# Attention with a gated MLP behind it: the first batch's LayerNorm spread tile by tile over two slots, and weight splits and copies placed elsewhere

## The chip, the cores and the metric

The kernel runs on one core of one Trainium2 chip, as one program. The metric is device time in microseconds: the median of several executions. Beside it stands one execution taken with the hardware profiler, from which all rows below come. TensorE is called PE there, VectorE DVE, ScalarE ACT, GpSimd POOL and SyncE SP. All loads and stores of this kernel but one are issued by SP.

## The reference

Block-causal attention over 8 batches of 8 heads (sequence 576, head size 64), then a gated MLP on its output:

```
scores = q @ k.T / 8, masked by blocks of 64; attn = softmax(scores); x = attn @ v     # (8, 576, 512)
h = gelu_tanh(x @ w_in)                  # w_in 512 x 1024
u, v = h[..., :512], h[..., 512:]
v_n = (v - mean(v)) / sqrt(var(v) + 1e-6) * g_ln          # over the last axis
v_s = einsum('ts,bsd->btd', w_sg, v_n) + b_sg[None, :, None]   # w_sg 576 x 576
out = x + (u * v_s) @ w_out
```

`w_in` and `w_out` come in as 64-bit floats, everything else as 32-bit floats.

## The kernel before

**Arithmetic.** Products that need 32-bit accuracy are made of three matmuls: each operand is split into a high part (a copy rounded to the matmul's 32-bit format, `fp32r`) and a low part (the difference). So `x` has `xh` and `xl`, the weights have `wi_h` and `wi_l`, `wo_h` and `wo_l`, `ws_h` and `ws_l`. Weights of 64 bits are first turned into 32-bit ones by bit operations: for a pair of 128x256 blocks, two passes of ACT, then five of DVE, then two of POOL for the split. `load_weight` yields after each of these three parts; `weight_half` runs one part. The spatial weights (`ws`, five blocks) only need POOL's two passes; the last of the five also holds the bias row, with one pass of ACT and one of DVE.

**Slots.** A slot is one pair of heads of one batch; there are 32, four for a batch. In slot n, PE turns the probabilities of pair n (`turn`: tiles `pA`, `pB`, `pC`, copied to `ptA`, `ptB`, `ptC`; `turn_sums`: `pd`, `pe`, copied to `rb`), makes half of the scores of pair n+1 (`first`), the product with the values (`products`: `ob`), the other half of the scores (`second`), and in four holes between these the tiles of the feed-forward part (FF) of the batch before: `v_part` (five tiles `accv`), `u_part` (eight `accu`), `s_part` (eight `accs`) and `o_part` (eight `acco`). DVE takes the maxima of the scores (`negm`), ACT the exponents (`prob`), POOL splits q and k of pair n+2.

Slots 0 to 3 (`opening_slot`) have no FF. The first batch's FF lies in slots 4 to 7 (`middle_slot`): the v tiles in slot 4, u in slots 5 and 6, s in slot 7. What else runs there, and after which hole, is written out in `SCRIPT`: `script[0]`, `[1]` and `[2]` come after the first three holes, `[3]` and `[4]` around the split of q and k, `[5]` at the slot's end. `weigh(k)` runs k parts of the weights' work, `fetch(k)` issues the loads of the next k weight blocks, `run_side(k)` k steps of the LayerNorm, `run_gelu` a waiting Gelu.

**Order.** In the first eight slots every engine runs its instructions in the order in which the program writes them, so an instruction that waits holds all that is behind it on its engine. From slot 8 on only PE's order is fixed, and the framework's scheduler orders the others by its own estimate of times.

**Buffers.** All matmuls write to a pool of eight PSUM banks (`bank`); a new tile takes a bank whose last reader is done, or waits for one. One pass of the weights' conversion takes a bank too. `KINDS` gives the buffers in SBUF: the five v tiles and the high and low parts of the normalised ones share nine, the raw spatial blocks `xr` have two, `x` has two.

**LayerNorm.** For each of five row tiles: `moments` (DVE, two instructions), `centre` (DVE: subtract the mean, multiply by the gain); then `inverse_std` for all tiles at once (POOL, two instructions); then `scale` (ACT makes the high part, DVE the low one; for the tail tile three instructions of DVE, which also write `vone`). `vone` is an operand whose lower half is all ones, for the bias.

All instructions go through the small class `Engine`, so most rows of the profile have its line, L60; the tiles' names tell them apart.

Of the kernel before, what the change touches and what calls it, by code (L numbers as in the profile page):

```python
# [9 lines left out]
F32 = mybir.dt.float32  # L10
# [10 lines left out]
def kernel(  # L21
# [13 lines left out]
    B, H, D, S = qT.shape  # L35
# [41 lines left out]
    def page(dtype, n, name):  # L77
        tag, bufs = KINDS.get(name, KINDS["w"])
        return sp.tile([P, n], dtype, tag=tag, name=name, bufs=bufs)
# [106 lines left out]
    ws_l = cp.tile([P, NT, S], F32R, name="ws_l")  # L186
    g_bc = cp.tile([P, DH], F32, name="g_bc")
    vone = cp.tile([P, DH], F32R, name="vone")

    def split_weight(x, dh, dl):  # L190
        gpsimd.tensor_copy(dh, x)
        gpsimd.tensor_tensor(dl, x, dh.bitcast(F32), op=ALU.subtract)

    W = 256
    raws = deque()
    coming = deque()

    def fetch(k=1):
# [4 lines left out]
    def fetch_weight(src, c, fs, name):  # L203

        t = page(src.dtype, W, name)
        sync.dma_start(t, src[c * P : (c + 1) * P, fs])
        raws.append(t)

    def fetches(src, cols, name):
        for f in range(cols.start, cols.stop, W):  # L210
# [3 lines left out]
    def load_weight(src, off, cols, dh, dl, name, size):  # L214

        parts = [(c, f) for f in range(0, cols, W) for c in range(NC)]
        for k in range(0, len(parts), size):
            c, f = parts[k]
            f += off
            if size == 2:  # L220
                dst = [x[:, c : c + 2, f : f + W] for x in (dh, dl)]
            else:
                dst = [x[:, c, f : f + W] for x in (dh, dl)]
                if coming:
                    fetch()
            raw = [raws.popleft() for _ in range(size)]
            if src.dtype == F32:
                yield False
                yield False
                for j, x in enumerate(raw):  # L230
                    split_weight(x, dh[:, c + j, f : f + W], dl[:, c + j, f : f + W])
                yield True
                continue
            words = [x.bitcast(U32).rearrange("p (n t) -> p n t", t=2) for x in raw]
            if size == 2:
                m = page(U32, size * W, name)
            else:
                tm = sp.tile([P, 2 * W], U32, tag="pt", name="tm", bufs=5)
                t, m = tm[:, :W], tm[:, W:]
            for j, x in enumerate(words):  # L240
                scalar.activation(
                    m[:, j * W : (j + 1) * W].bitcast(F32),
                    x[:, :, 1].bitcast(F32),
                    AF.Abs,
                    scale=2.0**-112,
                )
            yield False
            if size == 2:
                t = page(U32, size * W, name)
                y = bank("w").bitcast(U32)  # L250
            else:
                y = t
            for j, x in enumerate(words):
                yj = y[:, j * W : (j + 1) * W]
                vector.tensor_scalar(yj, x[:, :, 0], 29, None, op0=ALU.logical_shift_right)
                vector.scalar_tensor_tensor(
                    yj, x[:, :, 1], 0x80000000, yj, op0=ALU.bitwise_and, op1=ALU.bitwise_or
                )
            vector.scalar_tensor_tensor(
                t, m, 3, y, op0=ALU.logical_shift_left, op1=ALU.bitwise_or  # L260
            )
            yield False
            t = t.bitcast(F32)
            if size == 2:
                t = t.rearrange("p (c n) -> p c n", c=size)
            split_weight(t, *dst)
            yield True

    def load_spatial():
        t = page(F32, S, "x")  # L270
        gpsimd.memset(t[BLK:, :DH], 1.0)
        vector.tensor_copy(vone[BLK:, :], t[BLK:, :DH])

        for j in range(NT - 1):
            split_weight(raws.popleft(), ws_h[:, j, :], ws_l[:, j, :])
            yield True

        j = NT - 1
        t, t2 = raws.popleft(), raws.popleft()
        gpsimd.tensor_copy(ws_h[:, j, :], t)  # L280
        gpsimd.tensor_tensor(
            ws_l[:BLK, j, :], t[:BLK, :], ws_h[:BLK, j, :].bitcast(F32), op=ALU.subtract
        )
        scalar.copy(ws_l[BLK:, j, :], t2[BLK:, :])
        vector.tensor_tensor(
            ws_l[96:97, j, :], t2[96:97, :], ws_l[96:97, j, :].bitcast(F32), op=ALU.subtract
        )
        yield True

    def fetch_spatial(j):  # L290
        t = page(F32, S, "xr")
        sync.dma_start(t, w_sgT[j * P : (j + 1) * P, :])
        raws.append(t)

    def fetch_ends():
        t = page(F32, S, "xr")
# [3 lines left out]
        gpsimd.memset(t2[BLK:, :], 0.0)  # L300
        sync.dma_start(t2[BLK : BLK + 1, :], b_sg.unsqueeze(0))
        sync.dma_start(t2[96:97, :], b_sg.unsqueeze(0))
        raws.extend((t, t2))

    def fetch_gain():
        sync.dma_start(g_bc, g_ln.unsqueeze(0).broadcast_to([P, DH]))
# [140 lines left out]
    class Values:  # L447
# [75 lines left out]
        def split(self):  # L523

            x = self.x
            hi, lo = page(F32R, S + TAIL, "xh"), page(F32R, S, "xl")
            vector.tensor_copy(hi[:, :S], x)
            gpsimd.tensor_tensor(
                hi[:, S:], x[:, S - TAIL :], hi[:, S - TAIL : S].bitcast(F32), op=ALU.subtract
            )  # L530
# [2 lines left out]


    side = deque()

    def run_side(k):

# [29 lines left out]
    def v_part(b, vv, vn, vn_t, u, g_s):  # L568
        need("v")
        x_s = xs[b]  # L570
        for st in range(NT):
# [15 lines left out]
            else:  # L587
                vt = sp.tile([P, DH], F32, tag="pt", name="vt", bufs=5)
                scalar.copy(vt[:TAIL, :], acc[BLK:, :])
                vector.tensor_tensor(x, acc[:TAIL, :], vt[:TAIL, :], op=ALU.add)  # L590
            yield "v"
        rs = sp.tile([P, NT], F32, tag="rs", name="rs", bufs=2)

        def moments(st):
# [33 lines left out]
                )  # L628

        side.append(("G", lambda: gelu(vv, last)))  # L630
        for st in range(NT):
            side.append(("V", lambda st=st: moments(st)))
        side.append(("V", inverse_std))
# [1 line left out]
            side.append(("V", lambda st=st: centre(st)))  # L635
        for st in (NT - 1, *range(NT - 1)):
            side.append(("V", lambda st=st: scale(st)))

    def u_part(b, vv, vn, vn_t, u, g_s):
        need("u")  # L640
# [111 lines left out]
    def opening_slot(n, va):  # L752
# [34 lines left out]
        if n == Q - 1:  # L787
            nv.inverse()
            split_qk(n + 2)
        return nx, nv  # L790

    def slot(n, va):
# [44 lines left out]
        return nx, nv  # L837

    def weigh(k=1):
        for _ in range(k):  # L840
            weight_half()

    SCRIPT = {
        4: (
            lambda: (fetch(2), weigh(1)),
            lambda: weigh(3),
            lambda: (fetch(2), weigh(3)),
            lambda: None,
            lambda: weigh(3),
            lambda: (fetch(3), weigh(2)),  # L850
        ),
        5: (
            lambda: (run_gelu(), weigh(1), fetch(1)),
            lambda: run_side(2),
            lambda: (run_side(3), weigh(1), fetch(1)),
            lambda: run_side(1),
            lambda: weigh(1),
            lambda: None,
        ),
        6: (  # L860
            lambda: (run_side(5), weigh(1), fetch(1)),
            lambda: (run_side(4), weigh(1)),
            lambda: run_side(1),
            lambda: None,
            lambda: fetch(1),
            split_pending,
# [11 lines left out]
    def middle_slot(n, va):  # L878
# [6 lines left out]
        va.turn("A1")  # L885
        if n != 2 * Q - 2:
            split_pending()
        hole(g[0])
        script[0]()
        va.turn("B0")  # L890
# [12 lines left out]
        if n % Q == Q - 1:  # L903
            va.split()
        else:
            pending.append(va.split)
        nv = Values(n + 1, nx)
        nv.inverse()
        script[3]()
        split_qk(n + 2)  # L910
        script[4]()
        hole(g[3])
# [6 lines left out]
    split_qk(0)  # L919
    load_qk(1)  # L920
    fetch(2)
    sc = Scores(0)
    sc.first()
    sc.second()
# [58 lines left out]
```

## Time and profile before

| | |
|---|---|
| median of 3 runs | 750.47 us (750.12 to 751.44) |
| the profiled execution | 748.33 us, of it a span of 746.5 us from first to last instruction |
| granted TensorE clock, mean | 0.995 |
| busy PE / DVE / ACT / POOL | 732.5 / 469.3 / 429.2 / 295.2 us |
| PE's longest waits | `ob` for ACT's `ptC` 3.1 us, `s` for DVE's `negm` 1.2, `s` for DVE's `ptB` 1.1, `accv` for POOL's `xl` 0.6 us |
| slots 4 to 7 | from about 52 to 140 us |

A row of the timeline has the start in us, the duration, engine, line, operation, tiles written and read, shape, a count where several were merged, and in brackets the idle time of the engine before it with what ended that. A row of the windows has, for each engine, its busy time and instructions in the stretch, then the granted clock, the DMA engines' mean busy share and GB/s.

### The profile page before, as it was taken

Reading aid. Unit: us, or ns where it says so; the run is one execution under the profiler, and the core shown is the slowest. Engines: PE = TensorE matmul, PEld = TensorE weight load, DVE = VectorE, ACT = ScalarE, POOL = GpSimd, SP = SyncE. Lnnn points to the kernel's source line nnn. Section 1 sums busy time; section 2 is a strip of 40 time slices with the busy share of each in tenths; the row PEclk is TensorE's granted clock in tenths of the full one; section 3 lists DMA queues with packets and bytes.
Section 4 is the critical chain, followed back from the end, with each engine's and each line's share of the span. In section 5 each row is a group of like instructions: output and inputs, shape, how many; then the busy total and the mean of one; then the engine's idle time right before and its main releaser. Section 6 shows DMA issues by size and latency. Waiting matters only on the chain.

```text
span 746.5 us, 18406 instructions
## 1 busy us (share of the span) xinstructions
PE 732.5 (98%) x6936; PEld 689.4 (92%) x6936; DVE 469.3 (63%) x1461; ACT 429.2 (57%) x1072; POOL 295.2 (40%) x360
## 2 busy tenths in 40 slices
PE   8999979999999999999999999999999999999998
PEld 6888879999998999989999899998999989998997
DVE  5997797778963487634866449554595446941732
ACT  6987768378632785437754487445873476722500
POOL 3866755645333343423435123452224432322121
PEclk9999989999999999999999999999999999999999
DMA  6566433334341223312252123521224221220032
GB/s 166 172 170 192 110 80 88 112 92 140 95 134 42 72 72 120 118 35 69 84 176 66 47 58 95 160 72 40 75 79 149 72 71 41 80 79 2 10 120 95
DMA packets 84299, 70.04 MB, mean 94 GB/s; under 512 B 59890, under 2 KB 59890, under 8 KB 84212
## 3 DMA queue, kind: packets, MB, share of 16 engines
q1 hardware_dynamic: 84068, 68.58, 31.6%
q8 instruction: 55, 0.90, 0.5%
q10 hardware_dynamic: 144, 0.29, 0.1%
q14 instruction: 32, 0.26, 0.1%
HBM read 49.98 MB, written 18.87 MB: 92 GB/s over the span
## 4 chain that ended last, share of the span: by engine, by line
PE 84%; DVE 7%; ACT 5%; issue 2%; DMA 1%; POOL 0%; ACTq 0%; DVEq 0%; POOLq 0%
PE accs L60 16%; PE acco L60 13%; PE accv L60 12%; PE accu L60 11%; PE s L60 10%; PE ob L60 10%; ACT prob L60 4%; PE pA L60 3%; PE pB L60 3%; PE pd L60 3%; PE pC L60 2%; DVE prob L60 2%; PE pe L60 1%; DVE vv L604 1%; DVE bs L598 1%
## 5 line engine op out<-in xcount | busy, mean ns | idle before, releaser
L60 ACT ACTIVATE prob<-prob,negm 128x576 f32<-128x576 f32 (+3 forms) x320 | 176.4, 553 | 60.1 <-DVE negm L60 58.8
L60 DVE CUSTOM_DVE_ANT_0 prob<-s,mask 128x256 f32<-128x256 f32 (+3 forms) x320 | 119.3, 417 | 44.0 <-PE s L60 41.4
L60 POOL TENSOR_TENSOR xh<-x,xh 128x64 fp32r<-128x64 f32 x32 | 10.5, 328 | 195.8 <-DVE xh L60 167.2
L60 POOL TENSOR_TENSOR gl<-u,gh 128x288 fp32r<-128x288 f32 x64 | 52.0, 816 | 90.2 <-DVE gh L60 73.9
L60 PE MATMUL accu<-xh,wi_h 128*128 128x288 f32 x256 | 78.3, 306 | 0.0
L60 PE MATMUL acco<-gh,wo_h 128*128 128x288 f32 x256 | 77.5, 303 | 0.4 <-DVE negm L60 0.2
L60 PE MATMUL accs<-ws_h,vh 128*128 128x288 f32 x256 | 77.9, 304 | 0.0
L60 PE MATMUL accs<-ws_h,vl 128*128 128x288 f32 x256 | 75.5, 295 | 0.0
L60 PE MATMUL accu<-xl,wi_h 128*128 128x288 f32 x256 | 75.5, 295 | 0.0
L60 PE MATMUL accs<-ws_l,vh 128*128 128x288 f32 x256 | 75.4, 295 | 0.0
L60 PE MATMUL acco<-gh,wo_l 128*128 128x288 f32 x256 | 75.4, 295 | 0.0
L60 PE MATMUL acco<-gl,wo_h 128*128 128x288 f32 x256 | 75.4, 295 | 0.0
L60 PE MATMUL accu<-xh,wi_l 128*128 128x288 f32 x256 | 75.4, 295 | 0.0
L60 PE MATMUL s<-kh,qh 64*128 64x320 f32 (+4 forms) x384 | 63.6, 321 | 3.4 <-ACT kh L60 1.2
L60 PE MATMUL accv<-wi_h,xh 128*128 128x512 f32 x160 | 65.3, 408 | 0.0
L60 DVE TENSOR_TENSOR u<-accs,u 128x288 f32<-128x288 f32 x64 | 29.2, 456 | 56.8 <-PE accs L60 55.1
L60 PE MATMUL accv<-wi_l,xh 128*128 128x512 f32 x160 | 62.8, 393 | 0.0
L60 ACT ACTIVATION_READ_ACCUMULATOR prob<-prob,negm 128x1 f32 x320 | 59.9, 187 | 0.0
L60 PE MATMUL s<-kh,ql 64*128 64x320 f32 (+4 forms) x384 | 59.1, 300 | 0.0
L60 PE MATMUL s<-kl,qh 64*128 64x320 f32 (+4 forms) x384 | 58.0, 299 | 0.3 <-DVE kl L60 0.3
L60 ACT COPY vv<-accv 128x512 f32<-128x512 f32 x32 | 18.6, 582 | 64.9 <-PE accv L60 64.9
L60 POOL CAST kh<-k_f 128x576 fp32r<-128x576 f32 x31 | 20.9, 674 | 75.7 <-PE s L60 75.7
(117 smaller groups left out, 2099.3 us busy)
## 6 DMA issues: line engine op xcount, KB each, us to landing
q_f<-in_qT SPq DMA_DIRECT2D x32, 288.0 KB, 3.4
spill<-x SPq DMA_DIRECT2D x32, 288.0 KB, 2.7
xr<-spill SPq DMA_DIRECT2D x32, 288.0 KB, 3.0
out_T<-xr SPq DMA_DIRECT2D x32, 288.0 KB, 3.4
k_f<-in_kT SPq DMA_DIRECT2D x31, 288.0 KB, 3.6
v_f<-in_v SPq DMA_DIRECT2D x32, 128.0 KB, 2.9
v_d<-in_v SPq DMA_DIRECT2D x64, 64.0 KB, 2.7
v_f<-in_v SPq DMA_DIRECT2D x64, 64.0 KB, 2.6
```

The costliest lines, as they stand in the source:

```text
L60: return lambda *a, **k: pin(method(*a, **k), self.letter)
L598: tc.keep_in_program_order(nc.vector.bn_stats(bs[:rows, :], x))
L604: tc.keep_in_program_order(nc.vector.scalar_tensor_tensor(x, x, stats[:rows, st, 0:1], g_bc[:rows, :], op0=ALU.subtract, op1=ALU.mult))
```

## The change

It rearranges what lies in slots 3 to 7, and changes no arithmetic:

- `vone`'s ones are made at the outset (memset on POOL, copy on DVE ahead of the first scores) and no longer in slot 5.
- The raw blocks wait in one queue for each kind, so that spatial blocks can be split before the u weights are done.
- One part of the u weights' conversion moves into slot 3, and those of slot 4 move forward; two spatial blocks are split in slot 4, two in slot 5 and the last, with the bias row, in slot 6. Their loads move forward with them.
- The first batch's LayerNorm is no longer run by `run_side`: `script` names its steps (`m` moments, `c` centre, `r` inverse deviation, `s` scale, each with its tile). Three tiles are centred in slot 5. The inverse deviation comes after the split of q and k in slot 5, where it came before it.
- The Gelu of v is issued at the start of slot 5, ahead of its first u tile; it was behind it. (`v_part` now yields after queueing the Gelu.) The Gelu of u stays at the start of slot 7.
- `script[3]` runs before the inverse of the sums, not after it.
- The copy that makes `xh` runs on ACT for pairs 3, 5 and 6; it ran on DVE. Pairs 5 and 6 are split at the end of slot 6.

```diff
--- before.py
+++ after.py
@@ -186,13 +186,15 @@
     ws_l = cp.tile([P, NT, S], F32R, name="ws_l")
     g_bc = cp.tile([P, DH], F32, name="g_bc")
     vone = cp.tile([P, DH], F32R, name="vone")
+    ones = page(F32, S, "x")
+    gpsimd.memset(ones[BLK:, :DH], 1.0)
 
     def split_weight(x, dh, dl):
         gpsimd.tensor_copy(dh, x)
         gpsimd.tensor_tensor(dl, x, dh.bitcast(F32), op=ALU.subtract)
 
     W = 256
-    raws = deque()
+    raws = {"w": deque(), "xr": deque()}
     coming = deque()
 
     def fetch(k=1):
@@ -204,7 +206,7 @@
 
         t = page(src.dtype, W, name)
         sync.dma_start(t, src[c * P : (c + 1) * P, fs])
-        raws.append(t)
+        raws[name].append(t)
 
     def fetches(src, cols, name):
         for f in range(cols.start, cols.stop, W):
@@ -223,7 +225,7 @@
                 dst = [x[:, c, f : f + W] for x in (dh, dl)]
                 if coming:
                     fetch()
-            raw = [raws.popleft() for _ in range(size)]
+            raw = [raws[name].popleft() for _ in range(size)]
             if src.dtype == F32:
                 yield False
                 yield False
@@ -267,16 +269,12 @@
             yield True
 
     def load_spatial():
-        t = page(F32, S, "x")
-        gpsimd.memset(t[BLK:, :DH], 1.0)
-        vector.tensor_copy(vone[BLK:, :], t[BLK:, :DH])
-
         for j in range(NT - 1):
-            split_weight(raws.popleft(), ws_h[:, j, :], ws_l[:, j, :])
+            split_weight(raws["xr"].popleft(), ws_h[:, j, :], ws_l[:, j, :])
             yield True
 
         j = NT - 1
-        t, t2 = raws.popleft(), raws.popleft()
+        t, t2 = raws["xr"].popleft(), raws["xr"].popleft()
         gpsimd.tensor_copy(ws_h[:, j, :], t)
         gpsimd.tensor_tensor(
             ws_l[:BLK, j, :], t[:BLK, :], ws_h[:BLK, j, :].bitcast(F32), op=ALU.subtract
@@ -290,7 +288,7 @@
     def fetch_spatial(j):
         t = page(F32, S, "xr")
         sync.dma_start(t, w_sgT[j * P : (j + 1) * P, :])
-        raws.append(t)
+        raws["xr"].append(t)
 
     def fetch_ends():
         t = page(F32, S, "xr")
@@ -300,7 +298,7 @@
         gpsimd.memset(t2[BLK:, :], 0.0)
         sync.dma_start(t2[BLK : BLK + 1, :], b_sg.unsqueeze(0))
         sync.dma_start(t2[96:97, :], b_sg.unsqueeze(0))
-        raws.extend((t, t2))
+        raws["xr"].extend((t, t2))
 
     def fetch_gain():
         sync.dma_start(g_bc, g_ln.unsqueeze(0).broadcast_to([P, DH]))
@@ -524,7 +522,7 @@
 
             x = self.x
             hi, lo = page(F32R, S + TAIL, "xh"), page(F32R, S, "xl")
-            vector.tensor_copy(hi[:, :S], x)
+            copy("a" if self.n in (Q - 1, 2 * Q - 3, 2 * Q - 2) else "v", hi[:, :S], x)
             gpsimd.tensor_tensor(
                 hi[:, S:], x[:, S - TAIL :], hi[:, S - TAIL : S].bitcast(F32), op=ALU.subtract
             )
@@ -533,6 +531,7 @@
 
 
     side = deque()
+    norm = []
 
     def run_side(k):
 
@@ -588,7 +587,8 @@
                 vt = sp.tile([P, DH], F32, tag="pt", name="vt", bufs=5)
                 scalar.copy(vt[:TAIL, :], acc[BLK:, :])
                 vector.tensor_tensor(x, acc[:TAIL, :], vt[:TAIL, :], op=ALU.add)
-            yield "v"
+            if st < NT - 1:
+                yield "v"
         rs = sp.tile([P, NT], F32, tag="rs", name="rs", bufs=2)
 
         def moments(st):
@@ -628,6 +628,10 @@
                 )
 
         side.append(("G", lambda: gelu(vv, last)))
+        if b == PAIRS[0][0]:
+            norm.extend((moments, centre, inverse_std, scale))
+            yield "v"
+            return
         for st in range(NT):
             side.append(("V", lambda st=st: moments(st)))
         side.append(("V", inverse_std))
@@ -635,6 +639,7 @@
             side.append(("V", lambda st=st: centre(st)))
         for st in (NT - 1, *range(NT - 1)):
             side.append(("V", lambda st=st: scale(st)))
+        yield "v"
 
     def u_part(b, vv, vn, vn_t, u, g_s):
         need("u")
@@ -787,6 +792,7 @@
         if n == Q - 1:
             nv.inverse()
             split_qk(n + 2)
+            weight_half()
         return nx, nv
 
     def slot(n, va):
@@ -837,30 +843,45 @@
         return nx, nv
 
     def weigh(k=1):
+
         for _ in range(k):
             weight_half()
 
+    def spatial(k=1):
+
+        for _ in range(k):
+            next(next(g for p, g in weights if p == "s"))
+
+    def layer_norm(*steps):
+
+        moments, centre, inverse_std, scale = norm
+        for step in steps:
+            if step == "r":
+                inverse_std()
+            else:
+                {"m": moments, "c": centre, "s": scale}[step[0]](int(step[1]))
+
     SCRIPT = {
         4: (
-            lambda: (fetch(2), weigh(1)),
-            lambda: weigh(3),
             lambda: (fetch(2), weigh(3)),
-            lambda: None,
-            lambda: weigh(3),
-            lambda: (fetch(3), weigh(2)),
+            lambda: (fetch(5), weigh(3)),
+            lambda: weigh(2),
+            lambda: (weigh(1), spatial(2)),
+            lambda: weigh(1),
+            lambda: weigh(1),
         ),
         5: (
-            lambda: (run_gelu(), weigh(1), fetch(1)),
-            lambda: run_side(2),
-            lambda: (run_side(3), weigh(1), fetch(1)),
-            lambda: run_side(1),
-            lambda: weigh(1),
+            lambda: (fetch(2), layer_norm("m0", "c0")),
+            lambda: layer_norm("m1", "c1", "m2", "c2"),
+            lambda: (layer_norm("m3"), spatial(2)),
+            lambda: layer_norm("m4"),
+            lambda: (layer_norm("r"), fetch(1)),
             lambda: None,
         ),
         6: (
-            lambda: (run_side(5), weigh(1), fetch(1)),
-            lambda: (run_side(4), weigh(1)),
-            lambda: run_side(1),
+            lambda: (layer_norm("c3", "c4"), spatial(1)),
+            lambda: layer_norm("s4", "s0", "s1"),
+            lambda: layer_norm("s2", "s3"),
             lambda: None,
             lambda: fetch(1),
             split_pending,
@@ -885,6 +906,7 @@
         va.turn("A1")
         if n != 2 * Q - 2:
             split_pending()
+        run_gelu()
         hole(g[0])
         script[0]()
         va.turn("B0")
@@ -904,9 +926,9 @@
             va.split()
         else:
             pending.append(va.split)
+        script[3]()
         nv = Values(n + 1, nx)
         nv.inverse()
-        script[3]()
         split_qk(n + 2)
         script[4]()
         hole(g[3])
@@ -919,6 +941,7 @@
     split_qk(0)
     load_qk(1)
     fetch(2)
+    vector.tensor_copy(vone[BLK:, :], ones[BLK:, :DH])
     sc = Scores(0)
     sc.first()
     sc.second()
```

## The prediction

> **What bounds the kernel.** I read the page's first two parts, then who waited for whom on PE, then PE's timeline over the first eight slots, and last the other engines' timelines at each place where PE stood.
>
> ```profile
> span 746.5 us, 18406 instructions
> PE 732.5 (98%) x6936; PEld 689.4 (92%) x6936; DVE 469.3 (63%) x1461; ACT 429.2 (57%) x1072; POOL 295.2 (40%) x360
> ```
>
> PE is busy for 732.5 of 746.5 us, so only its 14 idle us, and any stretch at a lower clock, can be won. The list of PE's waits puts the longest where the change acts, and the timeline gives the places:
>
> ```profile
> PE ob L60 <- ACT ptC L60: 3.1, 1, 3.1
> ```
>
> ```profile
> 55.83 0.50 PE L60 MATMUL accv<-wi_h,xl 128*128 128x512 f32 x1 [0.61 <-POOL xl L60]
> 64.41 0.39 PE L60 MATMUL s<-kh,qh 64*128 64x256 f32 x2
> 65.19 0.33 PE L60 MATMUL s<-kh,qh 64*128 64x320 f32 x2
> 66.00 1.09 PE L60 MATMUL ob<-ptA,v_f 128*64 128x128 f32 x16
> 70.16 0.50 PE L60 MATMUL accv<-wi_h,xh 128*128 128x512 f32 x1
> 83.00 0.39 PE L60 MATMUL s<-kh,qh 64*128 64x256 f32 x2
> 89.58 0.38 PE L60 MATMUL s<-kh,qh 64*128 64x320 f32 x1 [0.94 <-DVE negm L60]
> 90.81 0.39 PE L60 MATMUL accu<-xh,wi_h 128*128 128x288 f32 x1
> 100.65 0.39 PE L60 MATMUL s<-kh,qh 64*128 64x256 f32 x2
> 102.79 0.41 PE L60 MATMUL s<-kh,qh 64*128 64x320 f32 x1 [1.05 <-DVE ptB L60]
> 106.84 2.04 PE L60 MATMUL ob<-ptA,v_f 128*64 128x128 f32 x16 [3.09 <-ACT ptC L60]
> 113.07 0.40 PE L60 MATMUL accu<-xh,wi_h 128*128 128x288 f32 x1
> ```
>
> The same PE work, from the first scores of a slot to its last feed-forward tiles, takes 70.16-64.41 = 5.75 us in slot 4, 90.81-83.00 = 7.81 in slot 5 and 113.07-100.65 = 12.42 in slot 6. Slot 4 has no stall in that stretch, so slot 5 loses 2.06 us and slot 6 loses 6.67. Slot 6 loses more than its waits, because the clock fell:
>
> ```profile
> 104.00:106.00 2.00, 0.00 (x0) 0.00 (x0) 1.97 (x2) 1.21 (x2) 1.92 (x3) 0.56 0.00 0
> ...
> 110.00:112.00 2.00, 2.00 (x34) 1.93 (x32) 2.00 (x15) 1.77 (x6) 0.00 (x0) 0.73 0.00 0
> ```
>
> The last column but two is the granted clock. A mean of 0.56 and one of 0.73 put the half clock from about 104.2 to 111.1; PE worked from 106.84 on, 4.2 us of that, so 2.1 us of the 6.67 are the clock's.
>
> **The change, part by part.** Times below are those of the profiled execution (748.33 us with a span of 746.5), and the sum is carried over to the median of 750.47.
>
> *The outset.* A 64x512 memset and a 64x512 copy move out of slot 5 to where DVE waits for PE's first scores; price nothing.
>
> *End of slot 3: the copy to `xh` goes to ACT.*
>
> ```profile
> 52.39 1.59 DVE L60 CAST xh<-x 128x576 fp32r<-128x576 f32 x1
> 52.38 1.28 POOL L60 TENSOR_TENSOR wi_l<-w,wi_h 128x512 fp32r<-128x512 f32 x1
> 54.35 1.43 POOL L60 TENSOR_TENSOR xl<-x,xh 128x576 fp32r<-128x576 f32 x1
> 105.51 0.67 ACT L60 CAST ws_l<-xr 64x576 fp32r<-64x576 f32 x1
> ```
>
> ACT does such a cast in about 0.67 us, so `xh` is there at 53.1. POOL is held by `wi_l` until 53.66, and `xl` ends 0.35 us earlier. PE's 0.61 us wait falls to 0.26. That gain is spent at once, as follows.
>
> *Slot 4: the conversion of the u weights runs one hole earlier.* Half of one conversion now sits in slot 3, so each later step is pulled up. ACT's two passes over the seventh pair of raw weights stood behind `ptC`, `rb` and the third v tile; now they stand ahead of `ptC`. The pair's loads are issued where they were, behind the loads of q and k for slot 6: the first two of these four.
>
> ```profile
> 61.35 1.81 SPq L60 DMA_DIRECT2D w<-in_w_in  x4
> ```
>
> ```profile
> 61.82 5.15 DMA w<-in_w_in
> ```
>
> ```profile
> 62.12 0.61 ACT L60 COPY ptC<-pC 128x512 f32<-128x512 f32 x1
> 66.47 0.99 ACT L60 ACTIVATE w<-w 128x256 f32<-128x256 f32 x2 [1.36 <-DVE negm L60]
> ```
>
> The second load lands at 61.82+5.15 = 66.97, and ACT's two passes ended at 67.46. ACT will come to them at about 61.2 and be held until 67.46; `ptC`, at 62.12 before, ends near 68.0. DVE is held as well (its part of the same conversion now precedes the maxima), so both halves of the first scores, the third v tile, `pd`, `pe` and a weight bank stay occupied. That is seven of eight banks, with `pC`'s the first to come free. PE then stands in the second pair of scores from 65.0 to 68.0. The rest of that pair takes 66.00-65.19 = 0.8, so `ob` starts at 68.9 instead of 66.00: **+2.9**. The maxima end some 3.5 us later, but PE needs their exponents only at the next slot's turns. After an idle of 3.0 us I expect the half clock again: 2.1 us were lost in slot 6, nothing at the least; nearer to the first, I take **+1.3**.
>
> Here a page can be weighed. The rows above have the half clock after 1.05 and 3.09 us of idle, and it began at 104.2, only half a microsecond into the longer one. The Trainium skill, in "TensorE: Matmul & The Clock Gate", section "HAM oscillation — how this bites in real kernels", gives the rule as no idle gap longer than about 3.4 us. By that rule the 3.0 us gap here keeps the full clock and the sum below loses its 1.3; by the rows of slot 6, where neither gap reached 3.4, the clock falls, and I go by the rows.
>
> *Slot 5: statistics and centring tile by tile, Gelu of v one tile earlier, no `vone`.*
>
> ```profile
> 79.29 2.71 ACT L60 ACTIVATE vv<-vv 128x512 f32<-128x512 f32 x5
> 83.59 0.42 DVE L60 CAST vone<-x 64x512 fp32r<-64x512 f32 x1 [3.41 <-POOL x L60]
> 84.77 0.69 DVE L598 BATCH_NORM_STATS2 bs<-vv 128x6 f32<-128x512 f32 x1
> 96.58 5.55 DVE L604 SCALAR_TENSOR_TENSOR vv<-vv,stats,g_bc 128x512 f32<-128x512 f32 x5
> ```
>
> DVE stood 3.41 us for the memset that POOL reached late; that goes. Ahead of the maxima DVE now has four statistics (0.8 each with their aggregates) and three centrings (5.55/5 = 1.1 each), 6.5 us, against 4.0 before. They start as soon as Gelu delivers, where the stall was: its first tile ended at 79.29+2.71/5 = 79.8, comes 4.2 us later with slot 4's delay, and 1.7 earlier by one u tile (an estimate from the 9.84 us of four of them with the turns between, 90.81 to 100.65). From 82.3, with 6.5 us and `ptB` between (0.7), the maxima start at about 89.5, behind PE's scores at 83.00+4.2+1.6 = 88.8. PE needs the first banks back after `ob`, at about 92.5, and has them at 90.2, after two of the maxima: the 0.94 us wait and its smaller follower go, **-2.0**. If the passes are dearer by more than 2.3 us, PE waits for the rest.
>
> *Slot 6: two centrings, the scalings, the last spatial weight.*
>
> ```profile
> 104.77 0.72 ACT L60 ACTIVATE vh<-vv,rs 128x512 fp32r<-128x512 f32 x1 [4.78 <-DVE vn_t L60]
> 104.76 3.10 DVE L60 SCALAR_TENSOR_TENSOR vl<-vv,rs,vh 128x512 fp32r<-128x512 f32 x3
> ```
>
> Before, ACT stood 4.78 us for a page that DVE freed after five centrings, with `ptC` queued behind. Three centrings gone (3.3 us), that hold goes, but the bias row becomes late next. Its load is behind POOL's memset, now behind the split of q and k and the inverse deviation:
>
> ```profile
> 89.25 1.20 POOL L60 TENSOR_TENSOR rs<-rs,half 128x5 f32<-128x5 f32 x1
> 90.94 0.67 POOL L60 CAST qh<-q_f 128x576 fp32r<-128x576 f32 x1 [0.49 <-PE s L60]
> 93.80 1.43 POOL L60 TENSOR_TENSOR kl<-k_f,kh 128x576 fp32r<-128x576 f32 x1
> 100.33 0.57 POOL L60 MEMSET xr<- 64x576 f32 x1
> 100.93 0.61 SPq L60 DMA_DIRECT2D xr<-in_b_sg  x2
> ```
>
> ```profile
> v_d<-in_v SPq DMA_DIRECT2D x2, 16.0 KB, 1.9
> ```
>
> Counted from the end of the scores that free q and k: split 95.23-90.94 = 4.3, `rs` 1.5 with the add ahead of it, memset 0.6, issue 0.6, landing 1.9 (the fastest small load; at most 4.2, since ACT read the row at 105.51), ACT's copy 0.67: 9.6 us. Behind it on ACT stand `ptB`, a u copy, two `vh` and `ptC`, 2.7 us, so `ob` may start at 12.3. PE gets there after 100.65-90.81 = 9.84 of turns and u tiles and 1.6 of scores, 11.4: 0.9 us of stall. DVE has the bias subtraction (0.76), `ptB`, three passes over the tail tile, and four `vl` at 0.75 when POOL is idle, 6 us, then the first maxima: banks at 16.3 and 17.0, PE asks at 16: another 1.2. With 0.2 for banks, slot 6 loses 2.3 instead of 6.67: **-4.35**. With the landing at 4.2 it would be -2.1; with one that costs nothing, -6.2. SP's loads of v, q and k now queue behind the bias row, some 4 us later; v is wanted only 18 us on.
>
> *Slot 7.*
>
> ```profile
> 119.33 2.41 ACT L60 ACTIVATE u<-u 128x576 f32<-128x576 f32 x4
> ```
>
> Two `xh` copies (1.3 us) go to ACT ahead of the Gelu of u; the gate needs that Gelu before it frees `accs` banks. ACT's exponents end no earlier than before while PE is 2 us earlier: **+0.25**. Moving the output weights ahead of the inverse fills DVE's wait for the exponents; price nothing.
>
> **Sum:** 2.9 + 1.3 - 2.0 - 4.35 + 0.25 = **-1.9 us**. Everything later is bound by PE and only shifts. 748.33-1.9 = 746.4 in a profiled execution; 750.47-1.9 = **748.6** in the runs. A measurement of this kernel tells about 0.2% (1.5 us) from no change, so this lies just outside.
>
> **The rivals.**
> 1. *No stall in slot 4*: the pair lands before ACT asks, or PE has a free bank. For it: ACT was not held there before. Against it: landing at 66.97 and 61.2 on ACT. Without the 4.2 us: -6.1, **744.4**.
> 2. *The stall is there, the clock stays full* (the gap rule above, as a mechanism: 3.0 us is too short): -3.2, **747.3**. Against it: slot 6 dropped within two shorter gaps.
> 3. *Slower: the seventh pair lands later.* Seven loads are now issued in a row, not four. If they share the DMA engines evenly, the pair lands with the last.
>
> ```profile
> 65.00:66.00 1.00, 1.00 (x21) 0.96 (x17) 0.61 (x3) 0.11 (x1) 0.92 (x2) 1.00 1.02 371
> ```
>
>    At 371 GB/s (the last column) one load of 0.26 MB takes 0.7 us; five more loads than the pair itself are 3.5 to 4 us, and PE waits each of them: +1.9, **752.4**. It cancels the gain when the pair lands 1.9 us later, and is slower beyond 0.2% from 3.4. Against it: the second of four landed 5.15 us after its issue though two more followed it at once, and the three new ones come behind those.
> 4. *No difference*: slot 6's stalls, 0.9 and 1.2 us close together, bring down the clock there too (1.7 us): -0.2, **750.3**.
>
> **How the numbers follow.** Forecast 0.40 (own range 747.6 to 749.7; three quarters of it below 749.0, the bound of faster), rival 1 0.12, rival 2 0.08, rival 3 0.18, rival 4 0.22. Faster: 0.30+0.12+0.08 = 0.50; same: 0.10+0.22 = 0.32; slower: 0.18. The range cuts off most of rival 1 and the far side of rival 3: 745.6 to 752.2.
>
> **What would show it.** Right: in slot 4 ACT's passes over `w` end near 67.4 with `ptC` behind them, PE stands about 3 us at `s`, and the clock is half for some us after; in slot 5 no wait for `negm`; in slot 6 PE waits less than 1.5 us for `ptC` and about 1 us for `negm`, at full clock; the wait for `xl` near 0.26. Wrong: PE running through slot 4, or ACT's copy of the bias row beginning later than 10 us after the scores.

## The result, and the profile after

The kernel after takes **745.44 us** (median of 6 runs, 744.69 to 748.48) beside 750.35 for the kernel before in the same session (6 runs): a ratio of 0.9938, interval 0.9919 to 0.9956. It is faster by 0.6%, by more than twice the 1.9 us that were forecast and at the fast end of the range of 745.6 to 752.2: the ratio, taken of the 750.47 us from which the prediction started, gives 745.8. The profiled execution took 745.63 us. Its page and its list of PE's waits (us in total, times, longest):

```profile
span 743.8 us, 18397 instructions
PE 733.2 (99%) x6936; PEld 690.4 (93%) x6936; DVE 463.6 (62%) x1458; ACT 431.0 (58%) x1075; POOL 295.0 (40%) x360
```

```profile
PE s L60 <- ACT ptC L60: 2.5, 1, 2.5
PE s L60 <- DVE negm L60: 0.6, 2, 0.3
```

`ptC` still heads the list, with 2.5 us for 3.1, but it is another `ptC`: that of slot 4, which nothing delayed before. PE's timeline, first of before (the start of slot 4 and the first scores of slot 7), then of after:

```profile
52.66 0.48 PE L60 MATMUL accv<-wi_h,xh 128*128 128x512 f32 x1
125.55 0.38 PE L60 MATMUL s<-kh,qh 64*128 64x256 f32 x2
```

```profile
54.08 0.48 PE L60 MATMUL accv<-wi_h,xh 128*128 128x512 f32 x1
65.27 0.39 PE L60 MATMUL s<-kh,qh 64*128 64x256 f32 x2
68.91 0.41 PE L60 MATMUL s<-kh,qh 64*128 64x320 f32 x1 [2.54 <-ACT ptC L60]
73.96 0.50 PE L60 MATMUL accv<-wi_h,xh 128*128 128x512 f32 x1
86.81 0.39 PE L60 MATMUL s<-kh,qh 64*128 64x256 f32 x2
92.98 0.40 PE L60 MATMUL accu<-xh,wi_h 128*128 128x288 f32 x1
102.82 0.39 PE L60 MATMUL s<-kh,qh 64*128 64x256 f32 x2
104.88 1.16 PE L60 MATMUL ob<-ptA,v_f 128*64 128x128 f32 x16 [0.27 <-DMA v_f<-in_v]
109.08 0.38 PE L60 MATMUL s<-kh,qh 64*128 64x320 f32 x1 [0.34 <-DVE negm L60]
109.70 0.38 PE L60 MATMUL s<-kh,qh 64*128 64x320 f32 x1 [0.24 <-DVE negm L60]
110.31 0.40 PE L60 MATMUL accu<-xh,wi_h 128*128 128x288 f32 x1
122.78 0.38 PE L60 MATMUL s<-kh,qh 64*128 64x256 f32 x2
```

The row of `ob` at 104.88 names the load of `v_f`, but the loads of `v_f` next to it in time are those for slot 7; the load of the weights into PE for the same `ob` has ACT's `ptC`, which ended at 104.83:

```profile
104.88 0.92 PEld L60 LDWEIGHTS ob<-ptA,v_f 128*64 128x64 f32 x16 [0.39 <-ACT ptC L60]
```

The table has the stretches of the prediction (from a slot's first scores to the FF tiles behind its second ones; without a stall 5.75 us). Its row for slot 7 goes from the end of slot 6's stretch to slot 7's first scores; behind those both kernels take another 621.0 us (746.5-125.55 and 743.8-122.78). What lies between the rows is equal to 0.01 us:

| stretch | before | after | measured | forecast |
|---|---|---|---|---|
| v tiles of slot 4 up to the scores | 64.41-52.66 = 11.75 | 65.27-54.08 = 11.19 | -0.56 | in the next line |
| slot 4 | 5.75 | 73.96-65.27 = 8.69 | +2.94 | +2.9, `xl` included |
| half clock after it | - | none | 0 | +1.3 |
| slot 5 | 7.81 | 92.98-86.81 = 6.17 | -1.64 | -2.0 |
| slot 6 | 12.42 | 110.31-102.82 = 7.49 | -4.93 | -4.35 |
| up to slot 7's scores | 125.55-113.07 = 12.48 | 122.78-110.31 = 12.47 | 0 | +0.25 |
| sum | | | **-4.2** | -1.9 |

The medians differ by 4.9, which agrees with the 4.2 within the spread of the runs. The spans of the two profiled executions differ by only 2.7, since after's execution reached slot 4 1.42 us later (54.08 against 52.66). That part is not the change's: with the code of before at the start, experiment 8 got there at 54.17, and kernels with the changed start got there at 52.74 (experiment 4), 53.14 (experiment 10) and 53.55 (experiment 9). It goes with the moment at which the granted clock first came to full: 5.25 us in before's execution, 12.92 in after's, 12.85 in experiment 8's and 5.02 in experiment 4's.

### The profile page after: what moved, and what is told of

It is laid out like the page before. It is cut to its first block, busy times and chain, and to the rows that moved or that the text cites. A ratio compares the mean times of both kernels' runs of the same rounds, so it can differ in the third digit from the quotient of the medians.

```text
span 743.8 us, 18397 instructions
## 1 busy us (share of the span) xinstructions
PE 733.2 (99%) x6936; PEld 690.4 (93%) x6936; DVE 463.6 (62%) x1458; ACT 431.0 (58%) x1075; POOL 295.0 (40%) x360
## 4 chain that ended last, share of the span: by engine, by line
PE 87%; DVE 5%; ACT 2%; POOL 2%; issue 2%; DMA 1%; SPq 0%; ACTq 0%; DVEq 0%; POOLq 0%
PE accs L60 16%; PE acco L60 13%; PE accv L60 13%; PE accu L60 12%; PE s L60 11%; PE ob L60 10%; PE pB L60 3%; PE pA L60 3%; PE pd L60 3%; PE pC L60 2%; ACT prob L60 2%; PE pe L60 2%; DVE prob L60 1%; DMA w<-in_w_in 1%; DVE vl L60 1%
## 5 line engine op out<-in xcount | busy, mean ns | idle before, releaser
L60 PE MATMUL s<-kh,qh 64*128 64x320 f32 (+4 forms) x384 | 65.3, 327 | 4.7 <-ACT ptC L60 2.5
L60 PEld LDWEIGHTS s<-kh,qh 64*128 64x128 f32 x384 | 38.2, 189 | 15.4 <-issue 6.8
```

The costliest lines, as they stand in the source:

```text
L60: return lambda *a, **k: pin(method(*a, **k), self.letter)
```

## The experiments

**Slot 4: the seventh pair of raw weights.** ACT's rows of after, the issues on SP, and from the chain of waits in that stretch the load:

```profile
67.41 0.97 ACT L60 ACTIVATE w<-w 128x256 f32<-128x256 f32 x2 [5.41 <-DMA w<-in_w_in]
68.29 0.57 ACT L60 COPY ptC<-pC 128x512 f32<-128x512 f32 x1
```

```profile
62.31 1.81 SPq L60 DMA_DIRECT2D w<-in_w_in  x4
```

```profile
62.74 5.19 DMA w<-in_w_in
```

ACT stood 5.41 us for the load, with `ptC` behind it. Two ways to remove this were tried. *Experiment 1* puts ACT's passes behind `ptC` again, as before:

```diff
-            lambda: (fetch(5), weigh(3)),
-            lambda: weigh(2),
-            lambda: (weigh(1), spatial(2)),
+            lambda: (fetch(5), weigh(2)),
+            lambda: weigh(1),
+            lambda: (weigh(3), spatial(2)),
```

> Slot 4's steps are reordered so that ACT's passes over the seventh pair of raw weights come behind ptC, rb and the third v tile again, and DVE's part of that conversion behind the second maxima; the loads stay where they are. Theory (the order on ACT makes the stall of slot 4, 2.54 us at s for ptC): the stall goes and slot 4's stretch falls from 8.69 to about 5.8 us; but 2.6 us of DVE work now stand ahead of v's Gelu and the statistics of slot 5, so PE waits there for negm, 1 to 2 us: time 1 to 2 us under the changed kernel, ratio to before about 0.992. Rival (the bank that PE waits for is short whatever ACT does, because the scores' maxima are late): the stall stays within 0.5 us, ratio 0.994.

748.57 us, ratio 0.9983 (0.9974 to 0.9991): 3 us slower than after, where 1 to 2 us less was expected. The stall of slot 4 was gone (65.25 to 70.99, 5.74 us), but PE's and POOL's timelines show two new ones in slot 5, for POOL's `kh` and `kl` and not for `negm`:

```profile
85.37 0.39 PE L60 MATMUL s<-kh,qh 64*128 64x256 f32 x2 [1.45 <-POOL kh L60]
86.85 0.39 PE L60 MATMUL s<-kl,qh 64*128 64x256 f32 x2 [0.98 <-POOL kl L60]
```

```profile
75.24 0.61 POOL L60 CAST wi_h<-w 128x512 fp32r<-128x512 f32 x1 [9.44 <-DVE w L60]
84.18 1.13 POOL L60 CAST kh<-k_f 128x576 fp32r<-128x576 f32 x1
```

POOL stood 9.44 us for the weight pair that now came late, and the two spatial splits and the split of q and k are queued behind it. PE also stood 1.32 us for ACT's `prob` a little later, and the granted clock was half from 87.60 to 91.01. So the earlier place of the conversion is needed, once two spatial blocks stand behind it on POOL; what is wrong is only the time of its load. *Experiment 2* leaves the passes and issues the pair's two loads in slot 3:

```diff
-        fetch(2 if n < Q - 1 else 4)
+        fetch(2 if n < Q - 1 else 6)
         4: (
-            lambda: (fetch(2), weigh(3)),
+            lambda: weigh(3),
```

> The changed kernel with the loads of the seventh pair issued in slot 3, right behind the four weight loads there, instead of in slot 4; no other order is touched. Theory (ACT and DVE stand in slot 4 for the landing of that pair, at about 67.4): it lands by about 62.5, ACT's wait of 5.41 us and PE's 2.54 us go, and nothing is put off: 2.5 to 3 us under the changed kernel, ratio about 0.990. Rival (the DMA engines are the limit there, so that the loads of v, q and k pushed back by 0.5 MB make a stall instead): slot 4's stretch stays over 7.5 us, with PE waiting for a load; ratio 0.994 to 0.996.

742.04 us, ratio 0.9895 (0.9882 to 0.9908), an interval wholly below that of after. PE runs through:

```profile
64.97 0.39 PE L60 MATMUL s<-kh,qh 64*128 64x256 f32 x2
70.71 0.50 PE L60 MATMUL accv<-wi_h,xh 128*128 128x512 f32 x1
```

5.74 us for 8.69. The late load is shown to be the cause of the whole stall. It cost the changed kernel about 3 us: 2.9 in the two profiles from slot 4's start to slot 7's first scores, 3.4 by the medians, which are of two sessions.

**Slot 6.** In after, ACT still waits for the bias row, much less than feared:

```profile
101.42 0.67 ACT L60 CAST ws_l<-xr 64x576 fp32r<-64x576 f32 x1 [1.62 <-DMA xr<-in_b_sg]
```

*Experiment 3* issues the row's memset and load ahead of the inverse deviation:

```diff
-            lambda: layer_norm("m4"),
-            lambda: (layer_norm("r"), fetch(1)),
+            lambda: (layer_norm("m4"), fetch(1)),
+            lambda: layer_norm("r"),
```

> The changed kernel with the loads of the last spatial block and the bias row (and POOL's memset for them) issued ahead of the split of q and k in slot 5 instead of behind the inverse deviation. Theory (the bias row's landing holds ACT 1.62 us and DVE 2.31 us in slot 6, and PE's waits of 0.27, 0.34 and 0.24 us there follow from it): these waits go, slot 6's stretch falls from 7.49 to about 6.0 us; ratio about 0.992, 1.0 to 1.5 us under the changed kernel. Rival (slot 6 is bound by DVE's normalisation passes, not by the row): the stretch stays over 7 us, ratio 0.994.

746.02 us, ratio 0.9943 (0.9929 to 0.9957): the same as after. In its profile slot 6 took 111.74-104.94 = 6.80 us for 7.49, so the row's wait was worth 0.7; but the clock fell after the stall in slot 4 (below), which took 76.51-65.23 = 11.28 us for 8.69 and hid the gain in the time. *Experiment 6* makes the same edit on top of experiment 2, where that stall is gone:

> The pair loaded in slot 3 and the bias row's loads ahead of the split of q and k, both. Theory (the two waits are in different slots and add): slot 4's stretch 5.75 us as in e2_pair_loaded_sooner, slot 6's 6.8 as in e3_bias_row_sooner instead of 7.76: about 0.9 us under e2, 741.1 us, ratio 0.9885. Rival (what slot 6 gains is lost to POOL or DVE in slot 7): ratio 0.9895 as e2.

741.68 us, ratio 0.9894 (0.9878 to 0.9909). Slot 6 took 106.49-99.22 = 7.27 us; with experiment 2 alone it was 106.90-99.14 = 7.76. The 0.5 us is in the profile, while the times of the two can't be told apart. What remains, 1.5 us over a slot without a stall, has DVE's maxima as its only long waits (0.67 and 0.24 us for `negm`).

*Experiment 5*, on top of experiment 2, moves one scaling ahead of `ptC`:

```diff
-            lambda: layer_norm("s4", "s0", "s1"),
-            lambda: layer_norm("s2", "s3"),
+            lambda: layer_norm("s4", "s0", "s1", "s2"),
+            lambda: layer_norm("s3"),
```

> Base: the changed kernel with the seventh pair loaded in slot 3 (e2_pair_loaded_sooner, no stall in slot 4, 742.0 us). Here the scaling of tile 2 stands in script[1] of slot 6 again, so that ACT makes the third vh ahead of ptC, as before the change. Theory 1 (it was this place that made PE wait 3.09 us for ptC, whatever DVE does): ACT stands for a page until DVE is through the tail tile, ob starts about 1.8 us later, the stall for negm behind it goes, slot 6's stretch grows from 7.76 to about 8.4 us and the time by 0.6 us. Theory 2 (the centrings moved away free DVE early enough, so the place no longer matters): no wait of ACT for vh over 0.5 us, stretch and time within 0.3 us of the base.

743.14 us, ratio 0.9909 (0.9894 to 0.9925), an interval that overlaps experiment 2's; slot 6 took 107.86-99.31 = 8.55 us, 0.79 over experiment 2. PE's and ACT's rows show the old mechanism, a page that DVE frees late:

```profile
103.34 1.16 PE L60 MATMUL ob<-ptA,v_f 128*64 128x128 f32 x16 [1.99 <-ACT ptC L60]
```

```profile
102.09 0.72 ACT L60 ACTIVATE vh<-vv,rs 128x512 fp32r<-128x512 f32 x1 [0.99 <-DVE vn_t L60]
```

*Experiment 8* does the opposite move in the kernel before:

```diff
-            lambda: (run_side(4), weigh(1)),
-            lambda: run_side(1),
+            lambda: (run_side(3), weigh(1)),
+            lambda: run_side(2),
```

> The kernel before with one edit: in slot 6, the scaling of tile 2 moves from script[1] to script[2], behind ptC and rb. Theory 1 (its place on ACT made the 3.09 us): ptC is then held only by the bias row, PE's wait for it falls to about 0.8 us, but DVE's chain is as long as before and PE waits 2 to 3 us for negm instead: 1.6 us under before by PE's order, and up to 2 us more where the clock stays full; ratio 0.996 to 0.998. Theory 2 (DVE's five centrings are what costs): ratio within 0.001 of 1.

749.28 us, ratio 0.9988 (0.9974 to 1.0001). The wait of `ob` for `ptC` fell from 3.09 to 0.25 us, slot 6 from 12.42 to 113.51-102.14 = 11.37, and most came back as a wait for the maxima:

```profile
111.82 1.22 PE L60 MATMUL s<-kh,qh 64*128 64x320 f32 x2 [2.48 <-DVE negm L60]
128.37 0.39 PE L60 MATMUL s<-kh,qh 64*128 64x256 f32 x2
```

The 1.05 us are no gain, since the half clock moved. Before, it lay within slot 6 (104.24 to 111.07); here it lasted from 111.83 to 118.66, and PE took 128.37-113.51 = 14.86 us up to slot 7's scores, for 12.48 before. From slot 6's scores to slot 7's it was 26.23 us for 24.90, in an execution of 751.15 us. So the rows are those of theory 1 and the time is nearer to theory 2. The medians differ by 0.6 us (before took 749.92 in that session), which is not clear of noise: no gain from taking the page's wait off ACT alone is shown. Behind ACT's hold, DVE was late as well.

**Slot 5: which of the moves made room.** *Experiment 4* is after with the first three centrings back in slot 6:

```diff
-            lambda: (fetch(2), layer_norm("m0", "c0")),
-            lambda: layer_norm("m1", "c1", "m2", "c2"),
+            lambda: (fetch(2), layer_norm("m0")),
+            lambda: layer_norm("m1", "m2"),
...
-            lambda: (layer_norm("c3", "c4"), spatial(1)),
+            lambda: (layer_norm("c0", "c1", "c2", "c3", "c4"), spatial(1)),
```

> The changed kernel with the three centrings of slot 5 put back into slot 6 (all five stand there again, ahead of the last spatial block), statistics and everything else as changed. Theory 1 (tile by tile LayerNorm is what saves slot 6): DVE has 3 us more ahead of the maxima of slot 6, the stretch goes from 7.49 to about 10 us, ratio about 0.997. Theory 2 (DVE stands 2.31 us for the bias row in slot 6 anyway, so most of the centrings fit into that wait): the stretch grows by 1 us or less, slot 5 loses its last 0.4 us of delay, ratio 0.994 to 0.995; then the saving came from what was put behind ptC on ACT.

747.1 us, ratio 0.9960 (0.9945 to 0.9975). Slot 6 took 111.51-103.28 = 8.23 us (+0.74) and slot 5 took 93.44-87.70 = 5.74 (-0.43): a net of 0.3. The rest of the 1.7 us in the medians goes with the clock, which fell in its slot 4: that slot took 74.83-64.11 = 10.72 us for 8.69. *Experiment 11* is the same edit on top of experiment 2, without that fall:

> The version with the pair loaded sooner (742.04 us, 0.9895), with the first three centrings back in slot 6. Beside the run that moved them back in the changed kernel itself (747.1 against 745.44, of which its profile gave slot 6 only 0.74 us, and a fall of the clock in slot 4 the rest) this one has no stall in slot 4. Theory 1 (the early centrings are worth 0.7 us, and the rest was the clock): 742.7, ratio 0.9905, slot 6 at 8.5 us against 7.76. Theory 2 (they are worth the whole 1.7 us or more): 743.7 or more, ratio 0.992, with a new wait for `ptC` or `negm` of over 1.5 us in slot 6.

742.78 us, ratio 0.9911 (0.9895 to 0.9926); slot 6 took 107.63-99.33 = 8.30 us, 0.54 over experiment 2. So theory 1: the early centrings are worth half a microsecond, though the prediction rested most of slot 6's gain on them.

Then what brought the rest? Experiments 8 and 4 have the same LayerNorm passes in slot 6 and the same order behind `ptC`, and slot 6 takes 11.37 us in the one (0.8 of it the half clock from 111.83 on) and 8.23 in the other. Their five centrings on DVE, first in experiment 8, then in 4:

```profile
98.07 5.55 DVE L604 SCALAR_TENSOR_TENSOR vv<-vv,stats,g_bc 128x512 f32<-128x512 f32 x5
```

```profile
97.27 3.82 DVE L604 SCALAR_TENSOR_TENSOR vv<-vv,stats,g_bc 128x512 f32<-128x512 f32 x5
```

They begin 102.14-98.07 = 4.1 us ahead of PE's scores in the one and 103.28-97.27 = 6.0 in the other, and take 1.7 us less. In experiment 8 POOL splits two spatial blocks beside them (96.67 to 101.75) and one more beside the scalings; the change has moved four of the five to slots 4 and 5. 2.1 of the 4.93 us in slot 6 are the half clock that before had there. So the rest of slot 6's gain lies between the relief of DVE in slot 5 and the spatial splits that no longer run beside its passes; the two were not tried apart.

*Experiment 7*, on experiment 2, makes the ones in slot 5 again (memset and copy at the head of `script[0]`):

> Base as e5. The ones of vone are made at the start of slot 5 again, memset on POOL and copy on DVE ahead of the first statistics. Theory (slot 5's 2 us were DVE's wait of 3.41 us for that memset): POOL reaches the memset behind xl, DVE waits about 3 us, the maxima start about 3.4 us later and PE waits for negm again, 2 to 2.7 us: slot 5's stretch grows from 5.74 to about 8 us, time 2 to 3 us over the base, ratio about 0.993. Rival (slot 5 gained by the earlier Gelu and the tile by tile order): stretch under 6.5 us, ratio within 0.001 of 0.9895.

745.78 us, ratio 0.9954 (0.9939 to 0.9969): 3.7 us slower than experiment 2. DVE's rows and PE's:

```profile
84.14 0.42 DVE L60 CAST vone<-x 64x512 fp32r<-64x512 f32 x1 [5.47 <-POOL x L60]
```

```profile
87.78 0.76 PE L60 MATMUL ob<-ptB,v_f 128*64 128x128 f32 x9 [1.29 <-DVE ptB L60]
92.86 1.22 PE L60 MATMUL s<-kh,qh 64*128 64x320 f32 x2 [2.31 <-DVE negm L60]
```

Slot 5 went from 5.74 to 94.55-83.48 = 11.07 us, half clock included. The half clock went on to 99.53, so that PE took 106.68-94.55 = 12.13 us from there to slot 6's scores, for 99.14-89.29 = 9.85 in experiment 2; and slot 6 fell to 5.74, since slot 5's delay gave DVE time.

*Experiment 10*, on experiment 2, puts the Gelu of v behind the first u tile again:

```diff
-        run_gelu()
+        if n != Q + 1:
+            run_gelu()
         hole(g[0])
+        if n == Q + 1:
+            run_gelu()
```

> The version with the pair loaded sooner (742.04 us, 0.9895), with the Gelu of v of slot 5 again behind the first u tile. Theory 1 (slot 5 runs without a stall only because the Gelu comes early): statistics and centrings begin about 1.7 us later, the maxima of slot 5 too, from about 87.6 to 89.3, and PE waits up to 1.2 us for `negm` at the second pair of scores: 743.2, ratio 0.991, or 744 and more if the clock falls with it. Theory 2 (slot 5 lost its stall through the missing memset and copy of the ones alone, and has over 1.7 us of cover left): no wait over 0.2 us in slot 5, 742.0, ratio 0.9895.

743.44 us, ratio 0.9922 (0.9907 to 0.9936); slot 5 took 90.64-83.08 = 7.56 us (+1.8), with PE waiting where expected:

```profile
89.41 0.38 PE L60 MATMUL s<-kh,qh 64*128 64x320 f32 x1 [0.68 <-DVE negm L60]
90.04 0.38 PE L60 MATMUL s<-kh,qh 64*128 64x320 f32 x1 [0.24 <-DVE negm L60]
```

So theory 1 again: the removed `vone` alone doesn't do it, the early Gelu is needed as well.

**Slot 3's end: `xh` on ACT.** *Experiment 9*, on experiment 2, has every copy to `xh` on DVE:

> The version with the pair loaded sooner (742.04 us, 0.9895 of before), with all copies to `xh` on DVE again, as before the change. Theory 1 (the move of the copy at the end of slot 3 is worth PE's whole wait for `xl`, 0.61 us before and none after): that wait comes back at the second v tile of slot 4 with 0.4 to 0.6 us, and the two copies at the end of slot 6 are hidden on either engine: 742.5, ratio 0.990. Theory 2 (the moved copies are worth nothing: `xl` would be in time anyway, since `wi_l` ahead of it on POOL ends sooner): 742.0, no row with a wait for `xl`. Theory 3 (the copies also load DVE in slots 6 and 7, where its maxima are late): 743.5 or more, with a wait for `negm` in slot 7.

742.71 us, ratio 0.9911 (0.9896 to 0.9926), which is not told apart from experiment 2 by its time. The wait is there again, though (0.60 us, for 0.20 in experiment 2), and the v tiles up to the scores took 65.30-53.55 = 11.75 us, as before the change:

```profile
56.71 0.50 PE L60 MATMUL accv<-wi_h,xl 128*128 128x512 f32 x1 [0.60 <-POOL xl L60]
```

## Why the prediction was right in sign and too small

In slots 4 and 5 it came true by the mechanism it named; in slot 6 the size came near, but for the most part not for the reason given. The time is that of its second rival (the stall is there, the clock stays full: 747.3), with 1 us more from smaller terms. Of the 2.3 us between -1.9 and -4.2, 1.3 are the clock, 0.6 slot 6, 0.5 slot 4 and 0.25 slot 7, less 0.4 in slot 5.

**The clock, the step that failed.** The prediction said that after 3.0 us of idle the half clock comes "again". Stretches of 3.41 us, cut at the moments at which the granted clock changes in the trace, show what decides (length, PE busy with its count, the other engines, granted clock, DMA share, GB/s). First before, then after, cut in the same step from its own first change, and then experiments 3, 4, 5 and 7:

```profile
100.83:104.24 3.41, 1.87 (x24) 1.53 (x23) 3.36 (x6) 0.00 (x0) 0.74 (x2) 1.00 0.30 75
104.24:107.65 3.41, 0.81 (x8) 0.81 (x10) 3.38 (x4) 2.83 (x6) 1.76 (x2) 0.50 0.00 0
107.65:111.07 3.42, 3.42 (x40) 3.42 (x38) 3.30 (x12) 1.88 (x6) 0.00 (x0) 0.50 0.00 0
```

```profile
64.12:67.53 3.41, 2.25 (x19) 1.54 (x17) 0.13 (x1) 0.12 (x1) 1.57 (x2) 1.00 0.90 282
67.53:70.94 3.41, 2.03 (x33) 1.99 (x35) 3.20 (x12) 2.85 (x7) 0.79 (x2) 1.00 0.87 297
```

```profile
64.50:67.91 3.41, 1.83 (x17) 1.20 (x15) 0.83 (x2) 0.71 (x2) 1.21 (x1) 1.00 0.83 265
67.91:71.33 3.42, 2.75 (x23) 2.68 (x25) 3.25 (x15) 2.92 (x9) 1.53 (x2) 0.50 0.64 247
```

```profile
66.46:69.87 3.41, 1.74 (x27) 1.70 (x29) 3.08 (x10) 2.72 (x7) 0.61 (x1) 1.00 0.84 316
69.87:73.29 3.42, 3.42 (x44) 3.42 (x40) 1.79 (x12) 3.28 (x12) 3.26 (x4) 0.50 0.02 7
```

```profile
101.84:105.25 3.41, 1.91 (x38) 1.91 (x40) 2.44 (x5) 2.98 (x6) 0.00 (x0) 1.00 0.58 180
```

```profile
89.29:92.70 3.41, 1.27 (x18) 0.82 (x13) 3.31 (x11) 0.00 (x0) 0.00 (x0) 1.00 0.00 0
92.70:96.11 3.41, 3.23 (x12) 2.61 (x13) 3.41 (x19) 3.28 (x13) 1.34 (x2) 0.50 0.00 0
```

In these rows the clock is decided at the end of each stretch by what PE did in it. Behind 1.87, 1.83, 1.74 and 1.27 us of work it fell; behind 2.25, 2.03 and 1.91 it stayed. After's one gap of 2.54 us was cut in two by a boundary at 67.53 and left 1.16 and 1.38 us of idle on the two sides; experiment 3's gap, shorter at 2.25 us, lay with 1.58 us of idle in one stretch and cost the clock. So what the prediction took over from slot 6 is a matter of where the gap falls, and in after's runs it shows as a spread: four took 744.7 to 745.6 us at a mean clock of 1.0, one 748.48 at 0.995. Where the clock did fall behind this stall, it cost more than 1.3 us: PE worked at half for 3.42 us in experiment 4 and for 2.75 and 3.41 in the two stretches of experiment 3, of which 1.7 and 3.1 us are the clock's. The Trainium skill, "TensorE: Matmul & The Clock Gate", section "HAM oscillation — how this bites in real kernels", has the rule as no idle gap over about 3.4 us; 3.4 us agrees with the length of the stretches here, but 1.54 us of idle within one was enough (before), so the rule spares gaps that these rows show to cost the clock. So the prediction was right not to go by the rule, and wrong to put the fall into its sum and leave the full clock only 0.08.

**Slot 4.** Right in cause and place; 2.94-0.56 = 2.38 us net for 2.9. The move of `xh` to ACT left 0.2 us of the wait for `xl` (forecast 0.26). The loads were issued 62.31-54.08 = 8.23 us into the slot, for 61.35-52.66 = 8.69 before, half a microsecond sooner; the landing took 5.19 us for 5.15. Rival 3 (three more loads behind delay it) is refuted by that row, and rival 1 by the stall.

**Slot 5.** Counted from the slot's first scores (86.81; in the forecast 83.00+4.2), statistics began 4.7 us ahead (forecast 4.9) and the maxima 4.1 behind (forecast 2.3): the centrings took 2.02, 1.12 and 1.71 us, not 1.1 each.

```profile
83.03 2.02 DVE L604 SCALAR_TENSOR_TENSOR vv<-vv,stats,g_bc 128x512 f32<-128x512 f32 x1
86.50 1.12 DVE L604 SCALAR_TENSOR_TENSOR vv<-vv,stats,g_bc 128x512 f32<-128x512 f32 x1
88.48 1.71 DVE L604 SCALAR_TENSOR_TENSOR vv<-vv,stats,g_bc 128x512 f32<-128x512 f32 x1
90.92 0.39 DVE L60 CUSTOM_DVE_ANT_0 prob<-s,mask 128x256 f32<-128x256 f32 x1
```

The 1.8 us more are within the 2.3 that the prediction allowed, and yet 0.43 us of stall were left, so the allowance was too large. Experiment 4 removes the 0.43 by taking the centrings away; but experiment 2 removes them too with the centrings in place. There they took 0.97, 0.93 and 1.28 us, and the maxima began 86.00-83.55 = 2.45 us behind the scores:

```profile
86.00 0.39 DVE L60 CUSTOM_DVE_ANT_0 prob<-s,mask 128x256 f32<-128x256 f32 x1
```

**Slot 6.** The size came out near, but the reason given (three centrings gone, so the hold goes) covers little of it, as experiments 4 and 11 show: 0.74 and 0.54 us. The bias row is the next thing late, as said, but at the short end: its issue began at 99.68 and ACT had it at 101.42, 1.7 us. PE's stall before `ob` is 104.88-102.82-1.59 = 0.5 us (forecast 0.9, with 66.00-64.41 = 1.59 in the slot without a stall), that for the maxima 110.31-107.87-1.25 = 1.2 (forecast 1.2, with 70.71-69.46 = 1.25 in experiment 2's slot 4). The clock did not fall there, against rival 4: PE's longest single waits were 0.34, 0.27 and 0.24 us.

**Slot 7 and the outset** cost nothing that the profile shows; no run shows the 0.25 us.

## What to carry to other kernels

When a step is moved forward in a hand-ordered program, move its load forward too: an engine that reaches its load before it has landed holds everything behind it, here the copy that PE needed; two loads issued a slot sooner gave about 3 us, beside the 4.9 of the whole change. And price a step by what is queued behind it on every engine it passes: putting the conversion back behind `ptC` was worse than the stall, because POOL's split of q and k stood behind it. A wait removed on one engine buys little while another engine ends just behind it: in experiment 8 a wait of 3.09 us went, one of 2.48 came, and the time can't be told from that of before. And where stalls move the half clock, compare stretches up to a point at which it is over in both kernels.

## What the runs showed of the hardware

- Over the 13 traces, between the first 14 us and the last 10 us of the span, the clock fell after each stretch of 3.41 us in which PE was idle for 1.54 us or more (six times, 1.54 to 2.48), and after none with up to 1.51 (experiment 5, whose single gap of 1.99 us straddled a boundary). It came back after one stretch in which PE was busy throughout (experiment 4: 3.42 of 3.42), and stayed half for another one where PE was busy for 2.75, 3.23 or 3.38 us (experiments 3, 7 and 8). That the stretches are cut in the same step from the first change to the end is inferred from the distances between changes (before's full clock lasted from 5.25 to 104.24 us, 29.0 such stretches), not seen where no change occurs. In the first 14 us these figures do not hold: the clock came to full after 2.76 us of work in 3.41 (before, 1.84 to 5.25), and fell after 1.35 and 1.42 us of idle (experiment 4, 5.02 to 8.43; experiment 10, 5.04 to 8.45). So the 1.5 us are what these gaps showed, and no exact threshold.
- The same centring on DVE took 0.76 us on the mean of five with only the end of a split and small passes on POOL beside it (experiment 4: 3.82), 1.11 beside two spatial splits (experiment 8: 5.55), and up to 2.02 in slot 5 of after, beside the split of x and a spatial block. But in slot 5 of experiment 2, beside splits of k, of weights and of x, it took 0.93 to 1.28. That POOL is the cause was not tried by itself.

The best kernels of the study are those with the pair loaded sooner: 742.04 us (0.9895) and, with the bias row sooner as well, 741.68 (0.9894), not told apart.
